# A spectral layer plus a gated layer on one core: a padded weight pool, a mirrored order of block pools, and an inverse root in one operation

## The chip, the cores and the metric

The kernel runs on one core of one Trainium2 chip. The time is that of the whole execution on the device, in microseconds (us), the median of several runs. Five engines work side by side, each on its own queue of instructions: TensorE (PE, with its weight loads listed apart as PEld), VectorE (DVE), ScalarE (ACT), GpSimd (POOL) and SyncE (SP), which here only issues transfers (DMA).

## The reference

A layer norm (mean and variance over 640 columns, epsilon 1e-5, no gain) of x, 2048 tokens by 640, feeds two branches whose results are added to x:

```python
xn = _layernorm(x, axis=-1)
return x + _A_ref(xn, ...) + _B_ref(xn, ...)
# A: a = xn @ hid_re.T, b = xn @ hid_im.T ; y = seq_re @ a - seq_im @ b
# B: gate = xn @ W_gate ; up = xn @ W_up ; h = relu(gate) * up ; h @ W_down   (F = 1728)
```

All inputs are float32. A multiplies by 2048 x 2048 matrices along the sequence, B has a hidden width of 1728.

## The kernel before, in words

Every float32 operand is kept as a high part (rounded by ScalarE to fp32r) and a low part (the rest, subtracted by VectorE). A product is three matmuls: high by high, high by low, low by high (`mm3`, lines L131 to L133). `split` (L125, L126) makes the two parts. Matrices are cut in two by two blocks and combined by seven products with sums of blocks in place of eight; these are the names B11, T1, B21, T2, B22, T3, T4.

**Stage 1 (0 to about 410 us): layer norm and the products along the sequence.** The tokens come in eight groups of 256 (`SG` = 2 blocks of 128). For each group the statistics are made (`ln_stats`, L205 and L206 on VectorE), a first inverse root (`ln_first`, L211: square root on ScalarE, reciprocal on VectorE), the centred tokens (`ln_center`, L226, VectorE), their high part (`ln_high`, L232, ScalarE, scaled by the first inverse root), a step that refines the root (`ln_refine`, L219 to L222, four small VectorE instructions), and the low part (`ln_low`, L236, VectorE). The high and low tokens are the weights (stationary operand) of the matmuls, the tiles `xs_early` and `xs_late`; the moving operand is a chunk of the sequence matrix, loaded as `raw` and split into `cb`.

- `first_group` (L304) does this for group 0, block by block, with the first two chunks of the sequence matrix cut in halves: `high(c, j)` (L309, ScalarE) and `low(c, j)` (L310, GpSimd or VectorE) split half j of chunk c. `behind_vector` (L246) is a GpSimd instruction on one column that reads what VectorE wrote last, so that GpSimd starts behind it.
- `first_products` (L519, matmuls L527) multiplies block j of group 0 with chunks 0 and 1.
- `next_group` (L251) does the norm for groups 1 to 7; its chunk is rounded at L258 and its low part made at L256. `next_products` (L491, matmuls L498) multiplies it.
- In these functions `pin` keeps the instructions in the order in which the program gives them, on each engine.
- Before anything has arrived, 48 matmuls on a tile of zeros (`warm`, L113) run.

**Stage 2 (about 410 to 735 us): gate and up.** `gate_up(n)` for n = 0 to 25 (13 slices of F for each half q of the tokens, q = 1 first). Weights are the tile `gw`, moving operands the token sets in `xs_early` and in `sets_b`; PE, DVE and ACT keep the program's order. The last of it, `gate_up_rest(0, ...)`, is thirty matmuls with the small weight tile `wr` (pool `wr`), and beside them `lead_split` prepares the first unit of stage 3 in `gw`.

**Stage 3 (about 731 us to the end): projection.** `project(q)` for q = 1, then q = 0, goes through B11, T1, B21, T2, B22, T3, T4. Each has units (`HID_UNITS`, `F_UNITS` and an end). A unit has a `load`, a `prepare` and a `run`; `drive(4, 2)` issues a unit's load four units ahead of its run and its prepare two ahead. In this stage SP and GpSimd keep the program's order. `load` fetches the blocks (`get`, L1094: tile `rw`, from `pqd` at L1102 or `hd` at L1108) into one of four pools `raws0` to `raws3` of six buffers, one pool for each of the four blocks; which pool is given by `place` (L1096). The weights come in two ways: as a raw tile `wr` (pool `wraw`, L1155 and L1158) that `prepare` splits into `wt`, or, for T2, T3 and T4, already split from the scratch `wparts` into the tile `wd` (pool `wdir`, L1151; `wend`, L1139). `run` multiplies; short end units are L1210. The results are added to `y` (L1236) and stored.

The load of B11's unit 1 also fetches B11's unit 0 (`rw`), which T1 needs later; then comes its own `wr`. B11's unit 0 itself is the unit that `lead_split` has prepared.

**Space.** Pools are stacked from the left or from the right of the 128 partitions. The pools of stage 3 take the place of those of stage 2, and a tile waits for those that read or wrote what lay there. From the left, in bytes per partition from one common start: stage 2 has gw0 17408, stage 2 x 4096, r1 32768, then prep 2 x 12288, tmp 10240 (p1, u2, u3 of 2048 and oa of 4096), wr 5120, hob 2 x 4096, z 2 x 9728, stage3 2 x 4096, sets 32768. Stage 3 has wraw 4 x 3072, ring2 4 x 8192, wts 4 x 6144, then raws0 to raws3, 6 x 4096 each. From the right: in stages 1 and 2 the pool `early` with `xs_early` (40960) and a pad `edge` of `EDGE` = 480 bytes; in stage 3 ends 4 x 2048, y 10 x 2048, wdir 6 x 4096. A pool's first tile lies in its lowest buffer; the next ones are given out from the highest downwards.

Of the kernel before, what the change touches and what calls it, by code (L numbers as in the profile page):

```python
# [7 lines left out]
F32 = mybir.dt.float32  # L8
F32R = mybir.dt.float32r
AF = mybir.ActivationFunctionType  # L10
OP = mybir.AluOpType
# [47 lines left out]
def fnet_reglu_kernel(  # L59
# [46 lines left out]
    nc.scalar.activation(root_t, eps_t, AF.Sqrt)  # L106
# [101 lines left out]
    def ln_first(g, mv, js):  # L208

        mean, v, ve, sd, r0, t = (mv[:, js, i] for i in range(6))  # L210
        return nc.scalar.activation(sd, v, AF.Sqrt, bias=eps_t), lambda: nc.vector.reciprocal(r0, sd)  # L211
# [4 lines left out]
    def ln_refine(g, mv, js):  # L216

        mean, v, ve, sd, r0, t = (mv[:, js, i] for i in range(6))
        yield nc.vector.tensor_scalar(ve, v, EPS, None, op0=OP.add)  # L219
        yield nc.vector.scalar_tensor_tensor(t, r0, -0.5, ve, op0=OP.mult, op1=OP.mult)  # L220
        yield nc.vector.tensor_tensor(t, t, r0, op=OP.mult)
        yield nc.vector.scalar_tensor_tensor(stat[:, 1, g, js], t, 1.5, r0, op0=OP.add, op1=OP.mult)  # L222
# [20 lines left out]
    def pin(steps):  # L243
        return [tc.keep_in_program_order(i) for i in steps]
# [6 lines left out]
    def next_group(g, b, raw, before):  # L251

        xs, bs, mv = ln_tiles(g)
        js = slice(0, SG)
        cs = K14 if g < NH else slice(0, D)
        low = lambda engine, j: pin([engine.tensor_tensor(flat(b, 1)[:, j], raw[:, j], flat(b, 0)[:, j].bitcast(F32), op=OP.subtract)])  # L256
        pin(ln_stats(g, xs, bs, mv, js))
# [7 lines left out]
        root, inverse = ln_first(g, mv, js)  # L265
        pin([root])
        pin([ln_mean(g, mv, js)])

        def finish():
            pin([ln_center(xs, mv, 0, cs)])  # L270
            pin([inverse()])
            pin([ln_high(g, xs, mv, 0, cs)])
            pin([ln_center(xs, mv, 1, cs)])
            late["high"] = pin([ln_high(g, xs, mv, 1, cs)])[0].ins
            if before is None:
                for j in range(SG):
                    low(nc.vector, slice(j * CH, (j + 1) * CH))
            pin(ln_refine(g, mv, js))
            late["ln"] = pin(ln_low(g, xs, j, cs) for j in range(SG))[-1].ins
            if g < NH:  # L280
                late["a21"] = g, xs, mv
# [22 lines left out]
    def first_group(b):  # L304
# [11 lines left out]
        root, inverse = ln_first(0, mv, j0)  # L316
        pin([root])
        pin([ln_center(xs, mv, 0, d0)])
        pin([inverse()])
        high(0, 0)  # L320
# [12 lines left out]
        root, inverse = ln_first(0, mv, j1)  # L333
        pin([root])
        pin([ln_center(xs, mv, 1, K14)])
        pin([inverse()])
# [4 lines left out]
        behind_vector(last(1))  # L341
        low(0, 1, nc.gpsimd)
        low(1, 1, nc.gpsimd)
# [175 lines left out]
    def first_products(j, b):  # L519

        keys = [("e1", 0), ("e1", 1), "v1"]
        for v, cs in ((0, (0,)), (1, (0,)), (0, (1,)), (1, (1,)), (2, (0, 1))):
            for c in cs:
                for d, key in zip((0, 1, 4), keys):
                    if j == 0 and v == 0:
                        E[c, key] = bank()
                    pin([nc.tensor.matmul(E[c, key], xn_part(j, d)[v == 1], b[c][0][:, int(v == 2), j],  # L527
                                          start=j == 0 and v == 0, stop=False)])
# [558 lines left out]
    for n, b, side in (("wraw", 4, "left"), ("ring2", 4, "left"), ("wts", 4, "left"), *((f"raws{i}", 6, "left") for i in range(4)), ("ends", 4, "right"), ("y", 1, "right"), ("wdir", 6, "right")):  # L1087
        open_pools[n] = ctx.enter_context(tc.tile_pool(name=n, bufs=b, side=side, reuse_waits="tile"))

    units = [("hid", u) for u in HID_UNITS] + [("f", u) for u in F_UNITS] + [("end", (NF // 2,))]  # L1090
# [3 lines left out]
    def get(q, kind, u):  # L1094
        what, ks = units[u]
        place = (("B11", "B12", "B21", "B22").index(kind) + (3 if q == 0 else 0)) % 4  # L1096
# [223 lines left out]
```

## Time and profile before

| what | value |
|---|---|
| median of 3 runs | 1031.7 us (1031.12 to 1032.37) |
| the profiled execution | 1031.89 us |
| its span, first to last instruction | 1030.1 us |
| granted clock of TensorE in it | 1.00 |
| TensorE busy | 1023.6 us, 99% |
| VectorE, ScalarE, GpSimd busy | 818.1, 433.9, 124.8 us |

Reading it: a row of the timeline gives start, length, engine, line and operation, out<-in by the program's names, and in brackets the engine's idle time just ahead of it with what ended it. "waited for" rows give the total, the number of times and the longest wait. A busy TensorE is not TensorE at its peak, so its pace (time per matmul) is read beside its waits.

### The profile page before, as it was taken

The page shows a single profiled execution, that of the slowest core. Times are in us where ns is not written, and L with a number is a line of the kernel's source. Part 1 is how long each engine was busy: PE and PEld are TensorE (multiplying, and loading weights), DVE is VectorE, ACT ScalarE, POOL GpSimd, SP SyncE. Part 2 cuts the span into 40 slices and gives each one's busy share as a digit, 9 for nine tenths or more (in the row PEclk, how much of TensorE's full clock was granted, in tenths as well). Part 3 has the DMA queues.
Part 4 walks back from the last instruction along what each step waited for, and adds up shares of the span by engine and source line. Part 5 has one row for each costly group of instructions (what it writes and reads, how often), then busy time and mean ns, then how long its engine had stood idle before and what let it go on. Part 6 is the DMA issues. An engine that isn't in the chain of part 4 may idle for free.

```text
span 1030.1 us, 12551 instructions
## 1 busy us (share of the span) xinstructions
PE 1023.6 (99%) x4520; PEld 844.0 (82%) x4520; DVE 818.1 (79%) x1117; ACT 433.9 (42%) x552; POOL 124.8 (12%) x196
## 2 busy tenths in 40 slices
PE   9999999999999999999999999999999999999998
PEld 7888888888888888888888888888788888888886
DVE  7967987998989585888778988886597895767973
ACT  5554453343433333433336434443454434444432
POOL 3531001012110002411100000011000000000000
PEclk9999999999999999999999999999999999999999
DMA  7897734968969784763464766774699467995724
GB/s 299 293 340 263 265 122 164 337 221 265 359 217 346 297 328 158 251 210 139 153 234 154 255 241 240 253 282 161 237 406 306 134 246 233 305 319 175 241 89 136
DMA packets 90525, 249.12 MB, mean 242 GB/s; under 512 B 11232, under 2 KB 30752, under 8 KB 87776
## 3 DMA queue, kind: packets, MB, share of 16 engines
q1 hardware_dynamic: 72288, 174.66, 49.6%
q0 software_dynamic: 18176, 73.67, 19.4%
q8 instruction: 35, 0.57, 0.2%
q14 instruction: 26, 0.21, 0.1%
HBM read 185.63 MB, written 61.62 MB: 240 GB/s over the span
## 4 chain that ended last, share of the span: by engine, by line
PE 99%; DMA 0%; DVE 0%; ACT 0%; SPq 0%; issue 0%
PE ps L131 31%; PE ps L133 31%; PE ps L132 31%; PE ps L498 3%; PE ps L527 1%; PE ps L1210 1%; PE ps L113 1%; DMA wr<-in_hid 0%; ACT wt L125 0%; DVE y L1236 0%; SPq L1102 0%; DVE warm L109 0%; DVE eps_t L103 0%
## 5 line engine op out<-in xcount | busy, mean ns | idle before, releaser
L125 ACT ACTIVATE cb<-rw 128x1024 fp32r<-128x1024 f32 x83 | 81.8, 987 | 136.2 <-PE ps L133 90.8
L126 DVE TENSOR_TENSOR cb<-rw,cb 128x1024 fp32r<-128x1024 f32 x83 | 93.9, 1132 | 50.9 <-ACT cb L125 50.1
L125 ACT ACTIVATE cb<-raw 128x1024 fp32r<-128x1024 f32 x71 | 75.3, 1060 | 114.8 <-PE ps L133 108.4
L126 DVE TENSOR_TENSOR cb<-raw,cb 128x1024 fp32r<-128x1024 f32 x71 | 86.8, 1223 | 40.0 <-ACT cb L125 39.7
L131 PE MATMUL ps<-cb,wt 128*128 128x512 f32 x270 | 105.2, 389 | 1.1 <-ACT wt L125 1.1
L132 PE MATMUL ps<-cb,wt 128*128 128x512 f32 x270 | 105.0, 389 | 0.0
L133 PE MATMUL ps<-cb,wt 128*128 128x512 f32 x270 | 104.9, 389 | 0.0
L131 PE MATMUL ps<-xs_early,gw 128*128 128x512 f32 x260 | 101.2, 389 | 0.0
L133 PE MATMUL ps<-xs_early,gw 128*128 128x512 f32 x260 | 101.2, 389 | 0.0
L132 PE MATMUL ps<-xs_early,gw 128*128 128x512 f32 x260 | 101.1, 389 | 0.0
L122 ACT ACTIVATE gw<-z 128x1024 fp32r<-128x1024 f32 (+1 forms) x52 | 57.7, 1110 | 79.5 <-DVE z L833 78.5
L131 PE MATMUL ps<-cb,xs_late 128*128 128x512 f32 x232 | 90.2, 389 | 0.0
L132 PE MATMUL ps<-cb,xs_late 128*128 128x512 f32 x232 | 90.2, 389 | 0.0
L133 PE MATMUL ps<-cb,xs_late 128*128 128x512 f32 x232 | 90.2, 389 | 0.0
L131 PE MATMUL ps<-cb,xs_early 128*128 128x512 f32 x226 | 87.9, 389 | 0.0
L132 PE MATMUL ps<-cb,xs_early 128*128 128x512 f32 x226 | 87.9, 389 | 0.0
L133 PE MATMUL ps<-cb,xs_early 128*128 128x512 f32 x226 | 87.9, 389 | 0.0
L122 ACT ACTIVATE u<-ps 128x512 f32<-128x512 f32 x52 | 31.1, 598 | 88.8 <-PE ps L133 88.8
L843 DVE TENSOR_TENSOR gw<-z,gw 128x1024 fp32r<-128x1024 f32 (+1 forms) x52 | 64.8, 1284 | 1.3 <-ACT gw L122 1.2
L131 PEld LDWEIGHTS ps<-cb,wt 128*128 128x128 f32 x270 | 50.7, 188 | 12.0 <-ACT wt L125 1.5
L133 PEld LDWEIGHTS ps<-cb,wt 128*128 128x128 f32 x270 | 50.7, 188 | 10.6
L132 PEld LDWEIGHTS ps<-cb,wt 128*128 128x128 f32 x270 | 50.7, 188 | 10.4
(191 smaller groups left out, 2216.3 us busy)
## 6 DMA issues: line engine op xcount, KB each, us to landing
raw<-in_dft SPq DMA_DIRECT2D x94, 512.0 KB, 6.1
z<-in_wgu SPq DMA_DIRECT2D x26, 640.0 KB, 3.9
wd<-wparts SPq DMA_DIRECT2D x30, 512.0 KB, 6.4
wparts<-pw POOLq DMA_DIRECT2D x12, 1152.0 KB, 4.4
hd<-ob POOLq DMA_DIRECT2D x26, 512.0 KB, 3.5
rw<-hd SPq DMA_DIRECT2D x24, 512.0 KB, 7.2
tk<-in_dft SPq DMA_DIRECT2D x16, 512.0 KB, 6.8
set<-r POOLq DMA_DIRECT2D x16, 512.0 KB, 4.0
```

The source lines that it names most:

```text
L113: nc.tensor.matmul(ps[:, :P], warm, warm, start=True, stop=True)
L122: return nc.scalar.activation(o, i, AF.Copy)
L125: nc.scalar.activation(hi, src, AF.Copy)
L126: return nc.vector.tensor_tensor(lo, src, hi.bitcast(F32), op=OP.subtract)
L131: nc.tensor.matmul(ps, wh, mh, start=first, stop=False, skip_group_check=more)
L132: nc.tensor.matmul(ps, wh, ml, start=False, stop=False, skip_group_check=more)
L133: nc.tensor.matmul(ps, wl, mh, start=False, stop=last, skip_group_check=more)
L498: start["pe"] = pin([nc.tensor.matmul(E[0, key], xn_part(n * SG + j, d)[v == 1], b[:, int(v == 2), j], start=False, stop=n % NH == NH - 1 ...
L527: pin([nc.tensor.matmul(E[c, key], xn_part(j, d)[v == 1], b[c][0][:, int(v == 2), j], start=j == 0 and v == 0, stop=False)])
L843: tt(self.w[:, 1, cs], self.z[:, cs], self.w[:, 0, cs].bitcast(F32), op=OP.subtract)
L1210: nc.tensor.matmul(B[out], w[:, 0, v, oo : oo + P], b[:, 0, 0], start=False, stop=last and v == 1, skip_group_check=more)
```

## The change

It has four parts.

1. A pool `edge3` with one tile of 480 bytes per partition is opened on the right between `y` and `wdir`. Nothing writes or reads it.
2. `place` in `get` is mirrored: for q = 1, B11, B12, B21, B22 used raws0, 1, 2, 3 and now use 3, 2, 1, 0; for q = 0 they used 3, 0, 1, 2 and now use 0, 3, 2, 1.
3. The first inverse root is one ScalarE operation (`Abs_reciprocal_sqrt` with epsilon as its bias) in place of a square root and VectorE's reciprocal, and the refinement has three VectorE instructions in place of four. The function used ahead of all else, on `root_t`, changes with it.
4. The order in the head. In `first_group` the rounding of the first half chunk, `high(0, 0)`, comes ahead of the root of block 0; the subtraction `low(1, 1)` goes from GpSimd to VectorE, ahead of GpSimd's `low(0, 1)`, which now waits for it. `first_products` takes the low half of chunk 1 ahead of that of chunk 0. For group 1, `next_group` makes statistics and root block by block: the first block's root is ahead of the rounding of the chunk on ScalarE, the second's behind the first `ln_high`, and the mean comes last.

```diff
-    nc.scalar.activation(root_t, eps_t, AF.Sqrt)
+    nc.scalar.activation(root_t, eps_t, AF.Abs_reciprocal_sqrt)
...
     def ln_first(g, mv, js):
-        mean, v, ve, sd, r0, t = (mv[:, js, i] for i in range(6))
-        return nc.scalar.activation(sd, v, AF.Sqrt, bias=eps_t), lambda: nc.vector.reciprocal(r0, sd)
+        v, r0 = mv[:, js, 1], mv[:, js, 4]
+        return nc.scalar.activation(r0, v, AF.Abs_reciprocal_sqrt, bias=eps_t)
...
     def ln_refine(g, mv, js):
-        mean, v, ve, sd, r0, t = (mv[:, js, i] for i in range(6))
-        yield nc.vector.tensor_scalar(ve, v, EPS, None, op0=OP.add)
-        yield nc.vector.scalar_tensor_tensor(t, r0, -0.5, ve, op0=OP.mult, op1=OP.mult)
-        yield nc.vector.tensor_tensor(t, t, r0, op=OP.mult)
-        yield nc.vector.scalar_tensor_tensor(stat[:, 1, g, js], t, 1.5, r0, op0=OP.add, op1=OP.mult)
+        v, r0, t = (mv[:, js, i] for i in (1, 4, 5))
+        for o, i, by, op in ((t, v, EPS, OP.add), (t, t, -0.5, OP.mult), (stat[:, 1, g, js], t, 1.5, OP.add)):
+            yield nc.vector.scalar_tensor_tensor(o, i, by, r0, op0=op, op1=OP.mult)
...
     def next_group(g, b, raw, before):
+        parts_of = [slice(j, j + 1) for j in range(SG)] if g == 1 else [js]
+        roots = [lambda p=p: pin([ln_first(g, mv, p)]) for p in parts_of]
...
-        pin(ln_stats(g, xs, bs, mv, js))
+        for p in parts_of:
+            pin(ln_stats(g, xs, bs, mv, p))
+            if len(roots) > 1:
+                roots.pop(0)()
         pin([nc.scalar.activation(flat(b, 0), raw, AF.Copy)])
...
-        root, inverse = ln_first(g, mv, js)
-        pin([root])
-        pin([ln_mean(g, mv, js)])
+        if g != 1:
+            roots.pop()()
+            pin([ln_mean(g, mv, js)])
...
             pin([ln_center(xs, mv, 0, cs)])
-            pin([inverse()])
             pin([ln_high(g, xs, mv, 0, cs)])
+            while roots:
+                roots.pop()()
             pin([ln_center(xs, mv, 1, cs)])
             late["high"] = pin([ln_high(g, xs, mv, 1, cs)])[0].ins
+            if g == 1:
+                pin([ln_mean(g, mv, js)])
...
     def first_group(b):
         pin(ln_stats(0, xs, bs, mv, j0))
-        root, inverse = ln_first(0, mv, j0)
-        pin([root])
+        high(0, 0)
+        pin([ln_first(0, mv, j0)])
         pin([ln_center(xs, mv, 0, d0)])
-        pin([inverse()])
-        high(0, 0)
         pin([ln_high(0, xs, mv, 0, d0)])
...
         high(0, 1)
-        root, inverse = ln_first(0, mv, j1)
-        pin([root])
+        pin([ln_first(0, mv, j1)])
         pin([ln_center(xs, mv, 1, K14)])
-        pin([inverse()])
         pin([ln_high(0, xs, mv, 1, K14)])
         pin(ln_refine(0, mv, j1))
         high(1, 1)
         pin([ln_low(0, xs, 1, K14)])
-        behind_vector(last(1))
+        low(1, 1, nc.vector)
+        behind_vector(b[1][0][:, 1, 1, CH - 1 :])
         low(0, 1, nc.gpsimd)
-        low(1, 1, nc.gpsimd)
...
-        for v, cs in ((0, (0,)), (1, (0,)), (0, (1,)), (1, (1,)), (2, (0, 1))):
+        for v, cs in ((0, (0,)), (1, (0,)), (0, (1,)), (1, (1,)), (2, (1, 0))):
...
-    for n, b, side in (("wraw", 4, "left"), ("ring2", 4, "left"), ("wts", 4, "left"), *((f"raws{i}", 6, "left") for i in range(4)), ("ends", 4, "right"), ("y", 1, "right"), ("wdir", 6, "right")):
+    for n, b, side in (("wraw", 4, "left"), ("ring2", 4, "left"), ("wts", 4, "left"), *((f"raws{i}", 6, "left") for i in range(4)), ("ends", 4, "right"), ("y", 1, "right"), ("edge3", 1, "right"), ("wdir", 6, "right")):
...
+    pool("edge3").tile([P, EDGE // 4], F32, name="edge")
...
-        place = (("B11", "B12", "B21", "B22").index(kind) + (3 if q == 0 else 0)) % 4
+        place = (("B22", "B21", "B12", "B11").index(kind) + (q == 0)) % 4
```

## The prediction

> **What bounds the kernel now.** I read the page first: how busy each engine is, and what the chain that ended last consists of.
>
> ```profile
> span 1030.1 us, 12551 instructions
> PE 1023.6 (99%) x4520; PEld 844.0 (82%) x4520; DVE 818.1 (79%) x1117; ACT 433.9 (42%) x552; POOL 124.8 (12%) x196
> ...
> PE 99%; DMA 0%; DVE 0%; ACT 0%; SPq 0%; issue 0%
> ```
>
> TensorE is the bound, so time comes from two places only: a matmul that takes longer than its neighbours, or TensorE standing still. The waits of TensorE's weight loads, over the whole run, tell the second:
>
> ```profile
> PEld ps L131 <- ACT wt L125: 1.5, 1, 1.5
> ...
> PEld ps L498 <- ACT xs_early L232: 0.4, 1, 0.4
> ```
>
> The 1.5 us lies where the projection begins (near 736 us); the L498 row ends the first 16 us, in which shorter waits of the same kind lie. For the pace of matmuls I cut the projection of q = 1 and q = 0 into stretches by the tile that holds the weights. Columns: window, length, then busy time and count for PE, PEld, DVE, ACT, POOL, then clock, DMA share and GB/s.
>
> ```profile
> 822.08:845.89 23.81, 23.81 (x106) 19.71 (x105) 22.34 (x26) 8.98 (x11) 0.00 (x0) 1.00 0.69 247
> 805.29:822.08 16.79, 16.79 (x73) 13.49 (x72) 14.62 (x17) 9.03 (x11) 1.66 (x3) 1.00 0.64 192
> 845.89:879.01 33.12, 33.12 (x143) 26.56 (x142) 22.11 (x25) 15.64 (x18) 2.70 (x5) 1.00 0.75 230
> 951.78:968.57 16.79, 16.79 (x73) 13.49 (x72) 15.03 (x18) 9.10 (x11) 1.62 (x3) 1.00 0.62 191
> 992.38:1025.28 32.91, 32.91 (x142) 26.38 (x141) 17.00 (x19) 10.38 (x11) 2.71 (x5) 1.00 0.52 160
> ```
>
> The first row is B22, whose weights are `wt`: 105 matmuls in 23.81 us, 226.8 ns each. The other four are T2, T3 and T4, whose weights are `wd`: 16.79 / 72 = 233.2 ns, 33.12 / 142 = 233.2, again 233.2, and 32.91 / 141 = 233.4. The granted clock is 1.00 in all five, TensorE never idles in them, and both kinds have the same moving tile `cb`. The groups by form say the same, 389 against 395 ns, while the weight load itself lasts as long:
>
> ```profile
> L132 PE MATMUL ps<-cb,wt 128*128 128x512 f32 x270 | 105.0, 389 | 0.0
> L132 PE MATMUL ps<-cb,wd 128*128 128x512 f32 x140 | 55.3, 395 | 0.0
> L132 PEld LDWEIGHTS ps<-cb,wt 128*128 128x128 f32 x177 | 33.2, 188 | 6.8
> L132 PEld LDWEIGHTS ps<-cb,wd x140: 187/187/188, 805.3 to 1024.8; 128*128 128x128 f32 x140
> ```
>
> **The pad (`edge3`).** It adds no instruction; it moves the six `wd` buffers down by 480 bytes per partition. By the sizes of the right-hand pools, `ends` (4 x 2048) and `y` (10 x 2048) put `wd` at the top of the space minus a multiple of 512 bytes. `xs_early`, which lies under a 480 byte pad of its own, is at the top minus 480 minus a multiple of 512. So the two differ by 480 modulo 512, and the change gives `wd` the remainder that `xs_early` has. Matmuls with `xs_early` as weights have the 389 ns of `wt` (the page's groups). I take it that the remainder is the cause: it is what sets `wd` apart, and the slow pace begins and ends with that tile. Upper bound: each stretch less its count times 226.8 ns, 0.46 + 0.92 + 0.46 + 0.93 = **2.8 us**; lower bound 0. I take 2.8, as `xs_early` and `wt` are the nearest rows. What could hide it is VectorE: in the T2 stretches it works 14.62 and 15.03 of 16.79 us. At the faster pace a stretch takes 16.33 us, still longer, and behind it B22 leaves VectorE 23.81 - 22.34 = 1.5 us.
>
> The Trainium skill ("TensorE: Matmul & The Clock Gate", section "LDWEIGHTS (loading the stationary operand)") gives a weight load as the number of columns over 1.2, in ns, and has no address in it. By it 128 columns take 107 ns (an estimate from that page) whatever the tile; the rows have 187 to 188 for both tiles, and the matmul's pace differs all the same. By that rule the pad is worth nothing: the third rival below.
>
> **The order of the block pools.** B11 of q = 1 goes from `raws0` to `raws3`; B12, B21, B22 mirror likewise, and the reuse of q = 1's pools by q = 0 stays pair by pair (B11 takes B22's). At issue is what the first loads of the projection wait for on SP's queue, here SP's waits, its queue, the transfer that the chain of work passes through, then PE, ACT and DVE:
>
> ```profile
> SPq L1102 <- DMA wend<-pw: 23.0, 1, 23.0
> SPq L1102 <- DVE ob L856: 8.4, 1, 8.4
> SPq L1102 <- PE ps L133: 3.5, 1, 3.5
> ```
>
> ```profile
> 718.81 12.63 SPq L1102 DMA_DIRECT2D rw<-pq  x2
> 731.49 0.43 SPq L1155 DMA_DIRECT2D wr<-in_hid  x1
> ```
>
> ```profile
> 731.49 4.06 DMA wr<-in_hid
> ```
>
> ```profile
> 723.88 0.39 PE L133 MATMUL ps<-sets_b,gw 128*128 128x512 f32 x1
> 730.68 0.39 PE L133 MATMUL ps<-xs_early,wr 128*128 128x512 f32 x1
> 735.01 0.39 PE L133 MATMUL ps<-gw 128*128 128x512 f32 x1
> 736.47 0.50 PE L131 MATMUL ps<-cb,wt 128*128 128x512 f32 x1 [1.07 <-ACT wt L125]
> ```
>
> ```profile
> 731.60 1.05 ACT L125 ACTIVATE cb<-rw 128x1024 fp32r<-128x1024 f32 x1
> 735.57 0.84 ACT L125 ACTIVATE wt<-wr 128x768 fp32r<-128x768 f32 x1 [2.92 <-DMA wr<-in_hid]
> 736.45 0.96 DVE L126 TENSOR_TENSOR wt<-wr,wt 128x768 fp32r<-128x768 f32 x1 [2.54 <-ACT wt L125]
> ```
>
> The second `rw` load (B11's unit 0, needed only by T1) waits first for `ob` (L856), then for the last matmul that reads the old weights `wr`, 730.68. By the sizes, the last buffer of `raws0` straddles `oa` and that `wr`. Behind it in the queue stands the urgent load, `wr<-in_hid` for unit 1; it lands 4.1 us after 731.49, ScalarE rounds it at 735.57, and TensorE, due at 735.01 + 0.23 = 735.24, starts at 736.47. Cost: 1.23 us, and 0.10 in the step behind it (736.47 to 736.80 by the start of the next matmul): **1.3 us**.
>
> `raws3` lies over `sets_b` alone, whose last reader starts at 723.88. The two `rw` loads and `wr<-in_hid` then go out at about 724.3 to 725.5 and land by about 730, the two loads ahead of it included. Then ScalarE is next: `cb` ends at 732.65, `wt` 0.84 later at 733.5; VectorE finishes `wt` at about 734.8. Due is 735.24, and the low weights one or two matmuls later, so the cover is 0.5 us; if it failed, each tenth late would cost a tenth. I take the whole 1.3; bounds 0 (some other reader holds `sets_b`) and 1.3. SP issues the same transfers, only six microseconds earlier, while nothing else is waiting for data.
>
> **The head.** Rows of the first 16 us, all engines:
>
> ```profile
> 0.75 1.28 ACT L106 ACT_TABLE_LOAD   x1 [0.75 <-PEq L1313]
> 7.12 0.68 DVE L310 TENSOR_TENSOR cb<-raw,cb 128x512 fp32r<-128x512 f32 x1
> 8.88 0.44 DVE L226 TENSOR_SCALAR r<-r,mv 128x384 f32<-128x384 f32 x1
> 9.16 0.63 ACT L309 ACTIVATE cb<-raw 128x512 fp32r<-128x512 f32 x1 [2.12 <-DMA raw<-in_dft]
> 9.70 0.28 ACT L211 ACTIVATE mv<-mv,eps_t 128x1 f32<-128x1 f32 x1
> 10.21 0.62 ACT L232 ACTIVATE xs_early<-r,mv 128x384 fp32r<-128x384 f32 x1 [0.23 <-DVE mv L219]
> 11.82 2.56 POOL L310 TENSOR_TENSOR cb<-raw,cb 128x512 fp32r<-128x512 f32 x2
> 12.40 0.21 DVE L206 BATCH_NORM_AGGREGATE mv<-bs 128x2 f32<-128x12 f32 x1
> 12.77 1.06 ACT L258 ACTIVATE cb<-raw 128x1024 fp32r<-128x1024 f32 x1 [0.38 <-DMA raw<-in_dft]
> 13.52 1.08 DVE L226 TENSOR_SCALAR r<-r,mv 128x384 f32<-128x384 f32 x1
> 14.52 0.15 DVE L211 RECIPROCAL mv<-mv 128x2 f32<-128x2 f32 x1
> 14.71 1.12 ACT L232 ACTIVATE xs_early<-r,mv 128x384 fp32r<-128x384 f32 x2 [0.60 <-DVE mv L211]
> 15.38 3.96 PEld L498 LDWEIGHTS ps<-cb,xs_early 128*128 128x128 f32 x18 [0.42 <-ACT xs_early L232]
> ```
>
> Removed: nine reciprocals and nine of 36 refine steps on VectorE, about 0.16 us each; the inverse root costs what the square root did (0.28, same operands). The first token block starts earlier by some 0.4 us, but that is worth nothing: the second waits for a transfer (9.16). Behind that arrival the chain is rounding, root, `xs_early` rounding; without the reciprocal the last starts at 10.0 instead of 10.21. TensorE's wait for POOL goes as well: one of two POOL subtractions (1.28 each) becomes a VectorE one of 0.68, and the new order of products reads the POOL half last. So TensorE starts the second block at 10.0 + 0.62 = 10.65 and, with eighteen matmuls of 0.23 and 0.1 for the start, is through at 14.9.
>
> What then counts is group 1. VectorE comes to its statistics 0.4 us later (0.68 more, 0.2 less), so the first half's are ready at 12.61 + 0.4 = 13.0; ScalarE takes the first root at 13.0 and the 1.06 us rounding of `raw` behind it, so that rounding ends at 14.3 instead of 13.83. This is the added wait: behind the root on ScalarE stands only that rounding, and TensorE waits for it no earlier than for the tokens. VectorE's centring starts at 13.52 + 0.4 = 13.9. POOL starts 0.4 later too, but with one piece, and is done at 13.5, so I price the centring at the 0.44 that it took at 8.88 and not at the 1.08 beside POOL. The rounding of the tokens starts at 14.4 against 14.71: **0.3 us**. If the 1.08 stayed, it would start at 15.0: 0.3 us lost. Bounds: -0.3 and +0.45 (L498's 0.42 with what follows it). From 16 us on TensorE never stops, so what the head gains is kept.
>
> **Sum.** 2.8 + 1.3 + 0.3 = 4.4 us. The profiled execution took 1031.89 us around a span of 1030.1, 0.2 above the median of 1031.7; 1031.89 - 4.4 = 1027.5, and by the median **1027.3**.
>
> **The rivals.** *Another wait at the projection's start:* `wr<-in_hid` is held by something else, or VectorE's 0.5 us is not enough. For it: the first `rw` row's waits show that old transfers hold buffers there too. Against it: ScalarE and VectorE idle 2.92 and 2.54 us before that work. Time: 1031.7 - 2.8 - 0.3 = 1028.6.
>
> *The pad does nothing:* the slow pace comes with how `wd` is filled, by DMA straight from `wparts` and not by ScalarE and VectorE, or the pad ends up elsewhere, so the change does not do what it says. Against it: the operands of both kinds have one shape and one clock. Time: 1031.7 - 1.3 - 0.3 = 1030.1. The skill's rule above would give this. Both failing together: 1031.4.
>
> *Slower:* the inverse root does not share ScalarE's table with the copies. The trace has a single table load (1.28 us) for square root, copy, identity and relu together. If the new function needed its own, each of the four roots of the head would bring two loads, 10.3 us, less the waits of 2.12 and 0.38 that hide some: 7.8 us, and 1031.7 - 4.4 + 7.8 = 1035.1, later groups left out. It decides from the first copy that is not in that table.
>
> The Trainium skill ("ScalarE: Activation LUTs", section "Table sets: the hidden batching unit") says that cheap functions such as copy, identity and relu are in every set; the trace agrees for the square root's set, and none shows the other. By that page this rival cannot occur.
>
> **Chances.** Forecast 0.70 (own range 1026.4 to 1028.2: the head's bounds and the 0.6 us scatter of the runs), another wait 0.11, no effect of the pad 0.11, both 0.03, slower 0.05. The range takes in the first two: 1026.4 to 1029.3, with 0.19 left out. About 0.2% (2.1 us) is what can be told from no change here: below 1029.6 the first two and a little of the third, 0.83; within 0.12; slower 0.05.
>
> **What would show it.** Right: matmuls with `wd` at 389 ns and about 16.3 us per T2 stretch; no wait of TensorE for `wt` where the projection begins, and `wr<-in_hid` issued near 725; L498's first weight load near 15.05 (14.4 + 0.62) and one table load. Wrong: 395 ns still (pad), a wait there with another name (pools), centring of 1 us beside POOL (head), or a table load per root.

## The result, and the profile after

The changed kernel takes **1026.8 us** (median of 6 runs, 1026.65 to 1028.48), beside 1031.55 us for the kernel before (6 runs, 1031.0 to 1032.37). The ratio is 0.9957, with a 95% interval of 0.9944 to 0.9970: 4.75 us less. Forecast were 1027.3 us and 4.4 us. The profiled execution took 1026.76 us, its span is 1024.9 us.

The lines of after's page that answer to those of before: span, busy engines, shares of the chain that ended last.

```profile
span 1024.9 us, 12519 instructions
PE 1018.8 (99%) x4520; PEld 842.9 (82%) x4520; DVE 816.4 (80%) x1100; ACT 435.7 (43%) x553; POOL 124.3 (12%) x195
...
PE 99%; DMA 0%; ACT 0%; DVE 0%; SPq 0%; issue 0%
```

TensorE has the same 4520 matmuls and is still the whole chain, but it is busy 4.8 us less. Work was not taken away: it was paced faster and stood still less. The same stretches as before, one by one (window, length, busy time and count of PE, PEld, DVE, ACT, POOL, clock, DMA share, GB/s):

```profile
802.79:819.11 16.32, 16.32 (x74) 13.51 (x72) 14.74 (x17) 9.07 (x11) 1.66 (x3) 1.00 0.63 197
819.11:842.91 23.80, 23.80 (x107) 19.71 (x105) 22.21 (x26) 9.01 (x11) 0.00 (x0) 1.00 0.69 248
842.91:875.18 32.27, 32.27 (x144) 26.58 (x143) 22.09 (x25) 15.69 (x18) 2.71 (x5) 1.00 0.77 234
947.94:964.26 16.32, 16.32 (x74) 13.51 (x73) 14.87 (x17) 9.10 (x11) 1.63 (x3) 1.00 0.63 197
988.06:1020.10 32.04, 32.04 (x142) 26.38 (x141) 17.00 (x19) 10.42 (x11) 2.72 (x5) 1.00 0.52 164
```

The second row is the `wt` stretch, 23.80 us as before (23.81). The four `wd` stretches went from 16.79, 33.12, 16.79 and 32.91 to 16.32, 32.27, 16.32 and 32.04: 0.47 + 0.85 + 0.47 + 0.87 = 2.66 us. By form, the two kinds are now the same:

```profile
L132 PE MATMUL ps<-cb,wt 128*128 128x512 f32 x270 | 105.0, 389 | 0.0
L132 PE MATMUL ps<-cb,wd 128*128 128x512 f32 x140 | 54.5, 389 | 0.0
```

The waits of TensorE's weight loads:

```profile
PEld ps L529 <- ACT xs_early L230: 1.1, 2, 0.9
...
PEld ps L133 <- DVE gw L126: 0.3, 1, 0.3
PEld ps L500 <- ACT xs_early L230: 0.2, 1, 0.2
```

The 1.5 us row for `wt` is gone, and no row has taken its place at the start of the projection. SP's longest wait between 700 and 745 us, its queue there, then the rounding and subtraction of unit 1's `wt`, then TensorE where its first matmul starts:

```profile
SPq L1105 <- PE ps L133: 27.9, 1, 27.9
```

```profile
723.21 0.81 SPq L1105 DMA_DIRECT2D rw<-pq  x2
724.12 0.38 SPq L1158 DMA_DIRECT2D wr<-in_hid  x1
```

```profile
729.14 0.85 ACT L125 ACTIVATE wt<-wr 128x768 fp32r<-128x768 f32 x1 [0.25 <-DMA wr<-in_hid]
730.20 0.95 DVE L126 TENSOR_TENSOR wt<-wr,wt 128x768 fp32r<-128x768 f32 x1
733.88 0.39 PE L133 MATMUL ps<-gw 128*128 128x512 f32 x1
734.11 0.39 PE L131 MATMUL ps<-cb,wt 128*128 128x512 f32 x1
```

SP now stands before the first `rw`, for a matmul of TensorE (the last one that reads `sets_b` starts at 722.79 and has 0.39 us), and is free at 723.21; the urgent load is issued at 724.12 instead of 731.49. `wt` is complete at 731.15, 3.0 us ahead of the matmul that reads it, and that matmul follows the one ahead of it by 0.23 us, the plain step. In the head:

```profile
0.75 1.28 ACT L106 ACT_TABLE_LOAD   x1 [0.75 <-PEq L1316]
8.51 0.64 ACT L315 ACTIVATE cb<-raw 128x512 fp32r<-128x512 f32 x1 [1.53 <-DMA raw<-in_dft]
9.05 0.28 ACT L211 ACTIVATE mv<-mv,eps_t 128x1 f32<-128x1 f32 x1
12.32 0.29 ACT L211 ACTIVATE mv<-mv,eps_t 128x1 f32<-128x1 f32 x1 [0.78 <-DVE mv L206]
13.19 0.69 DVE L224 TENSOR_SCALAR r<-r,mv 128x384 f32<-128x384 f32 x2
13.64 0.62 ACT L230 ACTIVATE xs_early<-r,mv 128x384 fp32r<-128x384 f32 x1
14.31 1.67 PEld L500 LDWEIGHTS ps<-cb,xs_early 128*128 128x128 f32 x8 [0.22 <-ACT xs_early L230]
```

There is one table load, as before. Group 1's products (L500, before L498) start at 14.31 instead of 15.38, 1.07 us earlier where 0.3 was forecast; the row at 8.51 tells a part of why. The second token block waits for `raw<-in_dft`, and in this execution that came at 8.51, in that of before at 9.16. How much of the 1.07 us is the change is a question for the experiments.

### The profile page after: what moved, and what is told of

It reads as the page before. It is cut to its first block, busy times and chain, and to the rows that moved or that the text cites. A ratio compares the mean times of both kernels' runs of the same rounds, so it can differ in the third digit from the quotient of the medians.

```text
span 1024.9 us, 12519 instructions
## 1 busy us (share of the span) xinstructions
PE 1018.8 (99%) x4520; PEld 842.9 (82%) x4520; DVE 816.4 (80%) x1100; ACT 435.7 (43%) x553; POOL 124.3 (12%) x195
## 4 chain that ended last, share of the span: by engine, by line
PE 99%; DMA 0%; ACT 0%; DVE 0%; SPq 0%; issue 0%
PE ps L133 32%; PE ps L131 32%; PE ps L132 32%; PE ps L500 3%; PE ps L529 1%; PE ps L1213 1%; DMA raw<-in_dft 0%; DVE y L1239 0%; ACT cb L315 0%; ACT xs_early L230 0%; SPq L200 0%; ACT mv L211 0%
```

## The experiments

The theory is that of the prediction: three causes in three places, which add up (2.8 + 1.3 + 0.3). The rivals are that the pad's effect has another cause than the address of the weights, that the wait at the projection's start hangs on something else than the queue, and that the head gives nothing. The first three kernels each do one part alone.

### The pad alone

```diff
-... ("y", 1, "right"), ("wdir", 6, "right")):
+... ("y", 1, "right"), ("edge3", 1, "right"), ("wdir", 6, "right")):
+    pool("edge3").tile([P, EDGE // 4], F32, name="edge")
```

> The kernel before with the pad alone. Address theory: matmuls with wd at about 227 ns where they had 233.3, all 428 of them, so 2.7 to 2.8 us less (ratio 0.9973), and the wait of TensorE for wt at the projection's start stays at 1.5 us. Rival (the slow pace comes with how wd is filled): 233 ns still and no change of time. The head's gain in the changed kernel was 1.0 us in its profile where 0.3 was forecast; here the head is that of before, so its first weight load of L498 shows how far that moves without any change: the arrival theory expects it anywhere from 14.7 to 15.5 with the arrival of the fifth load, the order theory within 0.1 of 15.38.

Measured: 1028.77 us (11 runs) beside 1031.61 us (27 runs), ratio 0.9977 (0.9968 to 0.9985): **2.84 us**. The wait at the projection's start is untouched:

```profile
PEld ps L131 <- ACT wt L125: 1.7, 1, 1.7
```

By itself the pad is worth what was forecast; by the interval, 1.5 to 3.3 us.

The head is that of before here, yet its first weight load of L498 is not near 15.38:

```profile
14.73 1.26 PEld L498 LDWEIGHTS ps<-cb,xs_early 128*128 128x128 f32 x6
```

The rounding that waits for the fifth load starts at 7.83 in this profile, and at 7.87 and 7.83 in the two others with the old head below. So the start of group 1's products moves by 0.6 to 0.8 us with no edit near it, as the arrival theory had it, and the profile of before, with 9.16, is the odd one.

### The order of the pools alone

```diff
-        place = (("B11", "B12", "B21", "B22").index(kind) + (3 if q == 0 else 0)) % 4
+        place = (("B22", "B21", "B12", "B11").index(kind) + (q == 0)) % 4
```

> The kernel before with the mirrored order of the block pools alone. Queue theory: wr<-in_hid is issued near 725 in place of 731.5, TensorE doesn't wait for wt, 1.3 to 1.4 us less (ratio 0.9987); wd stays at 233 ns. Rival (the wait takes another name): under 0.3 us less.

Measured: 1030.05 us (11 runs), ratio 0.9988 (0.9979 to 0.9997): **1.56 us**. The matmuls with `wd` are as slow as before, the urgent load is early:

```profile
L132 PE MATMUL ps<-cb,wd 128*128 128x512 f32 x140 | 55.3, 395 | 0.0
```

```profile
723.57 0.81 SPq L1102 DMA_DIRECT2D rw<-pq  x2
724.48 0.38 SPq L1155 DMA_DIRECT2D wr<-in_hid  x1
```

The interval is 0.3 to 2.2 us, so this is not told apart from 1.3 by the times. The traces give a reason why it may be more: the wait removed is not the same in each execution. The weight load waits 1.5 us in the profile of before, 1.7 with the pad alone, 1.8 with the head alone; the matmuls lose 1.34, 1.53 and 1.67 us there, and nothing in this kernel's profile.

### The head alone

```diff
-        root, inverse = ln_first(0, mv, j0)
-        pin([root])
+        high(0, 0)
+        pin([ln_first(0, mv, j0)])
... and all else of parts 3 and 4
```

> The kernel before with the inverse root in one operation and the new order of the head, without the pad and without the mirrored pools. The sum theory (0.3 us from the order of work behind the same arrivals): 0.2 to 0.4 us less. The rival, after the profile of the changed kernel (L498's first weight load at 14.31 in place of 15.38): the head itself is worth 1.0 us. Which part is arrival is read from the start of the rounding that waits for the fifth load (9.16 before, 8.51 in the changed kernel): if the gain follows that arrival, L498 starts 6.2 us behind it before and 5.8 behind it here.

Measured: 1031.24 us (11 runs), ratio 0.9997 (0.9988 to 1.0006): 0.37 us, and the interval takes in no change. The three parts sum to 2.84 + 1.56 + 0.37 = 4.77, the whole gave 4.75. So the parts add up, though an agreement to 0.02 us is chance: each part has some 0.9 us of uncertainty to either side. The head's own 0.37 can be tested better in the trace. A fixed point far behind the head is the 2001st of the 4520 matmuls (matmuls counted in order of start). With the pad alone, and in the changed kernel, it is this row:

```profile
449.19 0.39 PE L133 MATMUL ps<-r,gw 128*128 128x512 f32 x1
```

```profile
448.72 0.39 PE L133 MATMUL ps<-r,gw 128*128 128x512 f32 x1
```

The four profiles with the old head put it at 449.81 (before), 449.19, 449.11 and 449.06. The nine with the new one, which differ only in what comes later, have 448.56 to 448.85, with a mean of 448.67. The profile of before is the one in which the transfers came late. Without it the head is worth 449.12 - 448.67 = **0.45 us**, and 0.6 of the 1.07 us in the two main profiles is chance.

Group 1's first weight load in this kernel:

```profile
14.05 2.00 PEld L500 LDWEIGHTS ps<-cb,xs_early 128*128 128x128 f32 x9
```

It comes 6.3 us behind the rounding that waits for the fifth load (7.71); with the pad alone it is 6.9. Written down were 5.8 here and 6.2 with the old head, and neither came: when the fifth load comes this early, the second block's root waits for VectorE's statistics and not for the load, so the start does not follow it.

The matmuls show what the 0.45 us is made of. The first product of group 0 starts at 6.12 to 6.22 in the three profiles with the old head and early transfers, at 5.80 to 6.10 with the new one (means 6.17 and 5.88): 0.28 us. Inside group 0, two steps of the old head lose 0.14 us together, beside the weight loads' waits for VectorE and GpSimd; in the new one they are gone. No matmul step is lost where group 1 begins in those three, so TensorE was not held by group 1's tokens there. They end only just in time (14.68 with the pad alone), so they had to come earlier too for the gain to be kept.

Part of the gain can be lost again further on. In this kernel's profile it was:

```profile
PEld ps L131 <- ACT ob L122: 0.4, 1, 0.4
```

```profile
449.65 0.60 ACT L122 ACTIVATE ob<-ps 128x512 f32<-128x512 f32 x1 [2.02 <-DMA hd<-ob]
```

ScalarE waits for a store of the buffer `ob`, and TensorE for ScalarE. Two more of the fourteen profiles have this stall, with 1.2 and 1.9 us of waiting of the weight load; the matmuls lose 0.3, 1.0 and 1.8 us in the three. The others, the changed kernel among them, have none. It comes and goes with the transfers of that moment, in kernels with the old head too.

### Is it the address, and which?

The pad's effect was shown; that it works through the start of `wd` was not. Six kernels answer that, all made from the changed one. The traces hold no addresses: every start below is worked out from the sizes of the pools, and counted from the place that the tile has in the changed kernel, which is taken as a multiple of 512. The places of single buffers follow from the order in which a pool gives them out. First, all six buffers of `wd` off a multiple of 512 again, at six different starts:

```diff
-pool("wdir").tile([P, 2 * 4 * P], ...)
+pool("wdir").tile([P, 2 * 4 * P + 8], ...)
```

> The changed kernel with 32 bytes more in each of the six wd buffers, so that they start at 320, 352, 384, 416, 448 and 480 bytes beyond a multiple of 512. If what counts is a multiple of 64 bytes, the buffers at 320, 384 and 448 run at 226.7 ns and those at 352, 416 and 480 at 233.3, half of the 428 matmuls slow, 1.4 us more than the changed kernel. If a multiple of 512 is needed, all six run at 233.3: 2.8 us more. If the address doesn't matter, all at 226.7.

Measured (one run): 1029.35 us. A T2 stretch, for 72 matmuls, is as before the change:

```profile
802.71:819.51 16.80, 16.80 (x74) 13.55 (x72) 14.38 (x17) 8.97 (x11) 1.66 (x3) 1.00 0.64 190
```

By buffer, the mean steps are 233.2, 233.7, 232.7, 234.3, 231.6 and 232.8 ns for starts of 320 to 480 above a multiple of 512: all are slow, and the kernel is 2.55 us above the changed one. So neither 32, 64 nor 128 is enough. `wd` is filled by DMAs, `wt` by ScalarE and VectorE, so `wt` was moved too:

```diff
-("wts", 4, "left"),
+("padl", 1, "left"), ("wts", 4, "left"), ("padr", 1, "left"),
+    for n in ("padl", "padr"):
+        pool(n).tile([P, 64], F32, name="edge")
```

> This kernel is the changed one with a pad of 256 B ahead of the pool wts and another behind it, so that the buffers of wt start at 256 above a multiple of 512 and all other pools are back at multiples of 512. The buffers of wt are filled by ScalarE and VectorE, not by DMA. Theory of the address (a split weight is slow on any start that is no multiple of 512, whoever fills it): the matmuls with wt as weights, which have had 226.7 ns each, go to about 233 ns, as wd did at 32 to 480 above a multiple of 512; some 830 of them by 6.6 ns are 5.5 us, so about 1032.3 us. Rival, the way in which the buffer is filled (only tiles that DMAs write are slow off their places): wt stays at 226.7 and the time at 1026.8. Rival, half a step is enough (256 is as good as 0): the same 1026.8; 320 to 480 were all slow, 256 itself was not run.

Measured: 1026.87 us (4 runs; 0.9951, 0.9936 to 0.9966), and every form with `wt` still at 389 ns. The theory as written down fell: 256 above a multiple of 512 costs `wt` nothing. Either 256 is enough, or only tiles that DMAs fill are slow. The moving operand `cb`, moved to 256 in the same way, does not count either:

```diff
-("ring2", 4, "left"),
+("padl", 1, "left"), ("ring2", 4, "left"), ("padr", 1, "left"),
... both pads of 256 B
```

> This kernel is the changed one with a pad of 256 B ahead of the pool ring2 and another behind it, so that the moving operands cb of the split matmuls start at 256 above a multiple of 512, and no weight moves. Theory that only the weights' start counts: the wt and wd stretches keep 226.7 to 227.1 ns and the time is 1026.8 us. Rival, each operand that TensorE reads wants a start on 512: all matmuls with cb (some 3,700 of the span) go to about 233 ns, which would be above 20 us: 1048 us or more.

Measured: 1026.8 us (4 runs; 0.9952, 0.9939 to 0.9966), all forms at 389 or 390 ns, as in the changed kernel. The pool serves the projection alone, some 1,260 matmuls and not the 3,700 written down, so the rival would have cost 8 us; it is out all the same. Since a start of 256 turned out to be harmless for weights, this says only that 256 is harmless for the moving operand as well; no other start of it was run. Two kernels settle the rest. One puts the buffers of `wd` at 0, 64, 128, 192, 256 and 320:

```diff
-pool("edge3").tile([P, EDGE // 4], ...)
+pool("edge3").tile([P, EDGE // 4 + 32], ...)
-pool("wdir").tile([P, 2 * 4 * P], ...)
+pool("wdir").tile([P, 2 * 4 * P + 16], ...)
```

> This kernel is the changed one with 64 B more in each buffer of wd and a pad of 608 B in place of 480, so that the six buffers of wd start at 0, 64, 128, 192, 256 and 320 above a multiple of 512, about 70 of its 424 matmuls each. wt did not mind a start at 256. Theory that half a step is enough (weights count in steps of 256): the matmuls at 0 and 256 have 226.7 to 227 ns, those at the other four about 233: 2.0 us above the changed kernel, 1028.8 us. Rival, a tile that a DMA fills wants a full multiple of 512: 256 is slow too, only 0 is quick, 1029.1 us. Third, any start in the lower half of 512 is quick: 0 to 256 quick, and 320 slow, as it was: 1027.3 us. The profile's matmuls by buffer tell these apart, not the time.

Measured: 1028.45 us (5 runs; 0.9963, 0.9950 to 0.9977), nearest the 1028.8 of the first theory. The windows of single buffers, in the order of the text below (12 matmuls each, in the last two rows 6):

```profile
803.86:806.58 2.72, 2.72 (x14) 2.25 (x12) 2.72 (x4) 1.06 (x1) 1.62 (x3) 1.00 0.28 104
806.58:809.38 2.80, 2.80 (x14) 2.26 (x12) 2.79 (x4) 1.06 (x1) 0.04 (x1) 1.00 0.94 266
810.77:813.52 2.75, 2.75 (x14) 2.25 (x12) 1.25 (x2) 1.17 (x2) 0.00 (x0) 1.00 1.01 354
813.52:816.32 2.80, 2.80 (x14) 2.25 (x13) 2.57 (x3) 2.80 (x5) 0.00 (x0) 1.00 0.14 52
816.32:819.11 2.79, 2.79 (x13) 2.24 (x12) 2.79 (x5) 1.30 (x2) 0.00 (x0) 1.00 0.71 176
847.10:848.49 1.39, 1.39 (x7) 1.13 (x6) 1.30 (x3) 1.06 (x1) 0.24 (x1) 1.00 0.83 289
848.49:849.85 1.36, 1.36 (x7) 1.13 (x6) 1.36 (x2) 0.00 (x0) 0.00 (x0) 1.00 0.76 217
```

Start 0: 2.72 / 12 = 226.7 ns. Start 320: 233.3. Start 192: 229.2, between the two. Start 128: 233.3. Start 64: 232.5, by this window. The last two rows are one buffer at 256, read right behind one at 320: its first six matmuls still have 231.7 ns, its last six 226.7. So **256 is enough for a tile that DMAs fill, too**, and behind a slow buffer the pace takes some six matmuls to come back (four to nine in the other passages of this kind in its trace). That is why the buffers at 0 and 256 have means of 229.8 in this mixture; the first one at 0, behind the quick `wt`, has 226.7 from its first matmul on. 192 and 448 are the quickest of the slow starts in the two kernels (229.2 and 231.6), which fits a period of 256 but does not show it. The slow windows have DMA shares of 0.94, 0.14 and 0.71 and the first, quick one 0.28: the load of the DMA engines does not sort them.

The other kernel puts `wt` at 320, 352, 384 and 416, at which `wd` was slow:

```diff
-pool("wts").tile([P, 2, 2, 3 * P], F32R, name="wt")[:, :n]
+pool("wts").tile([P, 12 * P + 8], F32R, name="wt")[:, : 12 * P].rearrange("p (k v n) -> p k v n", k=2, v=2)[:, :n]
... with pads of 320 and 64 B ahead of the pool and behind it
```

> This kernel is the changed one with the four buffers of wt at 320, 352, 384 and 416 above a multiple of 512 (32 B more in each, a pad of 320 B ahead and of 64 B behind), starts at which wd was slow; no other pool leaves its multiple of 512. ScalarE and VectorE fill wt. Theory of the address alone (the weights' start counts, whoever fills the tile): some 830 matmuls at about 233 in place of 226.7 ns, 5.3 us, so 1032.1 us. Rival, only tiles that DMAs fill are slow off their places: wt stays at 226.7 ns and the time at 1026.8 us.

Measured: 1032.48 us (10 runs; 1.0005, 0.9995 to 1.0014), 5.7 us above the changed kernel, where the theory had 5.3. A T2 stretch (`wd` on multiples of 512) and the B22 stretch (`wt`) are now the other way round:

```profile
804.72:821.08 16.36, 16.36 (x73) 13.52 (x72) 13.84 (x17) 9.01 (x11) 1.66 (x3) 1.00 0.63 184
821.08:845.58 24.50, 24.50 (x106) 19.73 (x105) 23.12 (x27) 8.98 (x11) 0.00 (x0) 1.00 0.69 248
```

16.36 / 72 = 227.2 ns for `wd`, 24.50 / 105 = 233.3 for `wt`. Who fills the tile does not matter; where it starts does. One thing these kernels do not separate: the moving operands stayed on their places, so it may be the weights' own start that counts, or its distance from that of the moving operand. Last, DMA writes to places off a multiple, with all operands of TensorE on theirs:

```diff
-*((f"raws{i}", 6, "left") for i in range(4)),
+("padl", 1, "left"), *((f"raws{i}", 6, "left") for i in range(4)), ("padr", 1, "left"),
... padl 480 B, padr 32 B
```

> This kernel is the changed one with the pools raws0 to raws3 at 480 above a multiple of 512, and all of wt, wd and cb on multiples of 512. TensorE doesn't read these pools; DMAs write them during the whole projection, in the T2 and T4 stretches little of it. Theory that a weight's own start counts: 1026.8 us, no pace changed. Rival, DMA writes to unaligned places load the memory and slow TensorE's reads beside them (then wd was slow because its own DMAs ran, not because it was read there): the wt stretches, where most of these loads run, go from 226.7 towards 233 ns, up to 5 us: up to 1032 us.

Measured: 1026.71 us (4 runs; 0.9946, 0.9930 to 0.9963), all forms with `wt` at 389 ns. This rival is out.

### Is it the queue?

The kernel before, its pools left alone, with the urgent `wr` of unit 1 issued ahead of the `rw` that held it:

```diff
     def load():
...
-                if name == "B11" and (q, "B11", 0) not in raws:
-                    get(q, "B11", 0)
...
                 if name in ("B11", "B21"):
                     nc.sync.dma_start(r, own[name == "B21"][:, :, : 3 * P])
...
+                if name == "B11" and (q, "B11", 0) not in raws:
+                    get(q, "B11", 0)
```

> This kernel is the one before, with the places of its pools kept, and only the order of two loads on SP's queue turned: the load of wr for unit 1 of the block B11 is issued ahead of that of rw for its unit 0, whose wait for a free buffer (12.6 us, to 731.49) held it. Theory that the queue's order makes the wait of 0.99 us at 735.01 and that the places only decide where the queue is stopped: wr of unit 1 goes near 719, the wait for wt at 735 is gone, and units 2 and 3, still issued behind 731, cost at most 0.7 us of it later, near 741: a gain of 0.7 to 1.4 us, 1030.1 to 1030.8 us. Rival, the place itself counts (which buffer lies where): the wait stays and the time is that of before, 1031.6 us.

Measured: 1030.47 us (11 runs), ratio 0.9989 (0.9980 to 0.9998): 1.24 us. SP's queue and TensorE:

```profile
719.88 0.34 SPq L1102 DMA_DIRECT2D rw<-pq  x1
720.31 0.39 SPq L1153 DMA_DIRECT2D wr<-in_hid  x1
732.20 0.80 SPq L1102 DMA_DIRECT2D rw<-pq  x2
```

```profile
742.40 0.43 PE L131 MATMUL ps<-cb,wt 128*128 128x512 f32 x1
742.82 0.50 PE L132 MATMUL ps<-cb,wt 128*128 128x512 f32 x1
743.15 0.40 PE L131 MATMUL ps<-cb,wt 128*128 128x512 f32 x1
```

The load of unit 1 passes the held one by 12 us, and the long step where the projection begins is gone. The later units still stand behind it, and the steps of 0.42, 0.34, 0.30 and 0.34 us from 742.40 to 744.02 (the first of them are shown) lose 0.5 us, near the place written down and within the 0.7 us given for them. The wait is the queue's; the place of the pools only decides where the queue is held, and until when. Mirroring the pools frees all units at once, and no such later steps are in its trace; by the times, 1.56 against 1.24 us, the two are not told apart.

### The operation or the order, in the head

The changed kernel with the old root back (square root, reciprocal, four refine steps), in the new order:

```diff
-        v, r0 = mv[:, js, 1], mv[:, js, 4]
-        return nc.scalar.activation(r0, v, AF.Abs_reciprocal_sqrt, bias=eps_t)
+        return nc.scalar.activation(mv[:, js, 3], mv[:, js, 1], AF.Sqrt, bias=eps_t)
+
+    def inverse(mv, js):
+        pin([nc.vector.reciprocal(mv[:, js, 4], mv[:, js, 3])])
... inverse(...) behind each ln_center of groups 0 and 1, once for the later ones
... root_t and the four refine steps as before
```

> This kernel is the changed one with the old inverse root back (square root on ScalarE, reciprocal and four refine steps on VectorE), while pad, order of pools and the head's new order stay. Theory that the operation is the smaller half of the head: ahead of the first rounding of group 1 a reciprocal stands again behind the centring, some 0.15 us as in the rows of before, and ahead of the second token block as well; the nine refine steps are hidden. L500's first weight load comes 0.15 to 0.3 us later against the arrival of group 1's tokens, and the time is 1027.0 us. Rival, the operation is all of the head's gain: 1027.2 us. Rival, the reciprocals are hidden and the order is all of it: 1026.8 us. The time alone can hardly tell these apart (0.2 us); the rows of the first 16 us are read beside it.

Measured: 1027.42 us (6 runs; 0.9968, 0.9957 to 0.9980), 0.6 us above the changed kernel: more than any of the three expectations. The rows around the start of group 1's products (here L509):

```profile
14.70 0.16 DVE L213 RECIPROCAL mv<-mv 128x1 f32<-128x1 f32 x1 [0.56 <-ACT mv L210]
14.78 1.27 DVE L260 TENSOR_TENSOR cb<-raw,cb 128x512 fp32r<-128x512 f32 x2
15.50 0.53 PEld L509 LDWEIGHTS ps<-cb,xs_early 128*128 128x128 f32 x3 [0.38 <-DVE cb L260]
```

The products start 0.34 us later (14.70 by the first matmul against 14.36), and then a weight load waits 0.38 us, which costs the matmuls another 0.22. The 2001st matmul comes at 449.36, 0.69 us behind the mean of the new head and 0.24 behind that of the old one. With the roots taken block by block, the second reciprocal waits 0.56 us on VectorE for ScalarE's root, and behind it stands the subtraction for `cb`, which TensorE needs next; in the changed kernel that subtraction starts at 13.80. So the operation is not an addend beside the order. It takes VectorE out of the way from the root to the rounding, and the order lives on that: in this form, order without operation gives back 0.6 of a head that is worth 0.4 to 0.5. The operation in the old order was not run.

### A step that is still there

The changed kernel's waits still show 0.3 us for `gw` near 730. The lead's split was put ahead of the relu and multiply of the last block:

```diff
+            if n and c == 0:
+                lead_split()
...
-            if n and c == 0:
-                lead_split()
```

> This kernel is the changed one with the lead step of the next weights' split issued ahead of the relu and multiply of the last block of gate and up, where the profile of the changed kernel still shows TensorE waiting 0.3 us for gw of VectorE near 730. Theory that VectorE's order makes this step: the 301 ns and 336 ns steps at 730 go, and the time falls by 0.2 us to about 1026.6 us. Rival: the multiply is then late itself, and as much is lost there: 1026.8 us, or up to 0.3 us more.

Measured: 1026.81 us (5 runs; 0.9951, 0.9939 to 0.9964), the same as the changed kernel's 1026.8. The row of 0.3 us is gone from the waits, and the profile's span is 1024.6 us, where the changed kernel and the three kernels of its pace have 1024.8 to 1025.1. The medians do not show the 0.2 us. The traces do: from the 2001st matmul to the last it is 571.19 us here and 571.37 to 571.40 in those four kernels, so the step went and was not lost elsewhere. It is smaller than what these times can tell, and no version here is shown to beat the changed kernel by them.

## Why the prediction was right

**The pad: right in place, cause and size.** 2.8 us was taken at the upper bound; 2.84 was measured by the times, and 2.66 by the four stretches. The argument from `xs_early`, that the remainder of the start is what sets `wd` apart, was not complete, since `wd` also differs from the others in being filled by DMAs; it holds all the same: moving `wt` to such starts makes it slow, and nothing else that was tried does. What it did not know is the step: 256 bytes, not 512. The weight load's own rows do not show the effect (187 to 188 ns for `wd` and for `wt` in every kernel here); it shows in the distance of the matmuls. By the Trainium skill ("TensorE: Matmul & The Clock Gate", section "LDWEIGHTS (loading the stationary operand)") a weight load's time depends on its columns alone. That rule does not foresee this. The Trainium skill ("SBUF — State Buffer", section "Operand start alignment") asks only for a multiple of the element's size; by the rows above a start on 64 B is allowed and costs 3%.

**The order of the pools: right mechanism, size perhaps too small.** Taken 1.3, measured 1.56 with an interval that holds 1.3. The term was read from one profile, in which the wait was 1.5 us; two other profiles with the old order have 1.7 and 1.8. The cover was sized far too small: `wt` was to be complete 0.5 us ahead of its matmul, and is 3.0 us ahead, since ScalarE rounds the weights at 729.14, ahead of `cb`, and not behind a `cb` that ends at 732.65. The first loads do wait for the last reader of `sets_b`, as forecast, and `wr` goes out at 724.12, where about 725 was given.

**The head: a size near the right one, in part by luck.** Taken 0.3 with bounds of -0.3 and 0.45; 0.37 by the times, with an interval that takes in zero, and 0.45 by the 2001st matmul. The term was worked out for an execution with late transfers, which the other profiles do not repeat. L500's first weight load was to be near 15.05 and is at 14.31. The forecast hung the chain on the arrival at 9.16; it came at 8.51, 0.65 us earlier, and 14.31 + 0.65 = 14.96. Group 1's root was forecast at 13.0 by the same chain and is at 12.32 + 0.65 = 12.97. For such late transfers the chain is therefore as forecast. But in the three other profiles with the old head no matmul step is lost where group 1 begins. The step that failed is the one that put the first token block's earlier start at nothing: that start is 0.28 of the 0.45 us, and 0.14 more are two stalls inside group 0 that the forecast does not name. That 0.3 us for group 1's tokens comes near the sum of these is chance. The choice that the centring costs 0.44 without POOL beside it, and not 1.08, held: two of them take 0.69 us together (13.19). What the sum did not see is that the new order needs the one operation, as the kernel with the old root showed.

**The rivals.** No other wait came at the projection's start; the pad works; the root needs no table of its own. The trace after has one ACT_TABLE_LOAD for all that ScalarE does, so copy, identity and relu came with the new function's table as well. The Trainium skill ("ScalarE: Activation LUTs", section "Table sets: the hidden batching unit") has such cheap functions in every set; the trace agrees. In that rival's sum eight loads of 1.28 us are 10.2 and not 10.3, which changes nothing.

**The sum.** 2.84 + 1.56 + 0.37 = 4.77 against 4.4, so the time is 0.5 us under the forecast, 0.26 of it from the pools and 0.15 from the kernel before, whose median was 1031.55 in these runs and 1031.7 in those shown first. The difference of the two profiled spans, 5.2 us, is more than that, since the profile of before had the late arrivals.

## What to carry to other kernels

Compare the distance of matmuls by the tile that holds the weights: two tiles of one shape at one clock with two paces point at where the tiles lie, and the dead pad was worth more here than either reordering. In a queue that keeps its order, look for the load behind the one that waits, and ask which old tile's last reader holds it; a different place for the pool moves that point. Before an effect of a few tenths at the start of a kernel is read from two profiles, compare the arrival of the first transfers in both, and use a fixed late matmul of several profiles as the clock. And price a start-up chain from more than one execution: which transfer or engine holds it can differ from one to the next.

## What the runs showed of the hardware

- Weights of 128 x 128 fp32r, moving operands of 512 columns, clock 1.00: 226.7 ns from matmul to matmul where the weights start 0 or 256 bytes above a multiple of 512 (counted from the places in the changed kernel), 229 to 234 ns at the nine other starts that were run (64, 128, 192, 320, 352, 384, 416, 448 and 480), whether DMA, ScalarE or VectorE wrote them. What in the chip makes this step was not found, nor whether the start of the moving operand has a part in it.
- The pace comes back late: behind a buffer at 320, some six matmuls with a buffer at 256 still had 231.7 ns. Where the slow `wt` is followed by a `wd` on its place, it takes five to nine.
- The weight load's recorded time does not show it: 187 to 188 ns in both cases.
- A store of `ob` that lands late near 450 us cost TensorE's matmuls 0.3, 1.0 and 1.8 us in three of the fourteen profiles, with no edit near it. A single profile can therefore carry almost 2 us that no part of a change has caused.
